# Which products of the first tile run on whole float32 operands, and a new order of the first 32 steps

## The chip, the cores and the metric

The kernel runs on one core of a Trainium2 chip, as one program with one launch. The metric is device time in microseconds, from the first to the last instruction with what the launch adds to it. The program is scheduled by a tool that writes each engine's instructions in a fixed order at build time; on the chip each engine goes through its own list in that order and waits for semaphores. The engines are named PE (matmuls; its weight loads are PEld), DVE (VectorE), ACT (ScalarE), POOL (GpSimd) and SP, whose queue issues nearly all DMAs here.

## The reference

Three stages follow each other; only the second is touched by the change.

```python
# 1: gated linear attention, 4 x 8 heads, 768 positions, head size 48
state = alpha[:, :, t, :, None] * state + einsum(k[:, :, t], v[:, :, t])
y[:, :, t] = einsum(q[:, :, t], state)
# 2: x is y as 3072 tokens x 384
h = x @ w_in                                  # 384 -> 2048
g = h * np.tanh(softplus(h))
x = g @ w_out                                 # 2048 -> 384
# 3: each token to the one expert of 8 with the largest logit
logits = x @ w_gate
out = gate * (np.maximum(x @ w1[e], 0.0) @ w2[e])
```

## The kernel before

**Attention units.** The 3072 tokens are cut into 24 units of 128 (unit u is u0, u1, ...). A unit is loaded by one DMA of 1 MB (`load_unit`, L339), goes through two scans and two products on DVE (`a_prep1`, `a_prep2`), a transpose on PE (`a_kt`), the products of q and k on PE with a masked copy `am` on DVE (`a_qk`), the sum `y` on PE (`a_y`), and the product that updates the state (`a_kv`). `a_y` ends in `xh`, a copy by ACT, and from the second tile on also in `xl`, what is left of float32 when `xh` is taken away, by DVE. `unit` has two buffers (unit 2 has one of its own), so the load of unit u+2 waits for `a_kv` of unit u on PE.

**Tiles and steps.** Three units make a tile of 384 tokens, 8 tiles in all. A tile is worked in 16 steps, one for each block f of 128 of the 2048 hidden columns. Step s (tile s // 16, block s % 16) is `mm1` (first product, into one of three PSUM buffers `h`), `act_tanh` and `act_mish` on ACT in batches of three steps, and six steps later `mm2` (second product, added up in `acc`). An `h` buffer is free when `tau` and the copy `hc` have been made from it: by ACT both in the first tile, `hc` by DVE (L659) in the others.

**Two ways of a product.** A float32 product is done either in one matmul with whole float32 operands, which PE runs as two recorded passes, or in three matmuls of the shorter type float32r on halves (high x high, high x low, low x high). Before, the first tile has whole operands in both products (L623 and L696), and the other seven have halves in both (L629, L701).

**Weights.** Block f of both weight matrices arrives as 64-bit numbers (`wraw`, 768 KB, two buffers, L346). `prep_w` makes float32 of them with three DVE instructions (`w_bits`, L66, L69, L72) into `wx[f]`. `prep_c` and `prep_d` turn the block of w_out on PE, multiply it with the gate's weights and put 8 more columns behind it (`wt`, `wot`, `wc`). `halve(f)` splits the whole of `wx[f]` into `w_h` (ACT, L429) and `wl` (DVE, L430), first at step 12.

**Order.** The first 32 steps or so follow a string of words written by hand: `a3` is `a_prep1(3)`, `b` `a_prep2`, `t` `a_kt`, `q` `a_qk`, `y` `a_y`, `v` `a_kv`, `l` a load, `w`, `c`, `d` the three preparations of a block, `m` a step, `s` `halve`, `z` one of four zero fills of `xs` (L799, 6.8 MB together), `P` the room for the second half of the weights. After the string a loop runs steps 16 on, with the later units between them. The words set the order in which the tool sees the work, and on SP's queue also the order of the DMAs. `craw` loads (L828) read the weights a second time for a check.

Of the kernel before, what the change touches and what calls it, by code (L numbers as in the profile page):

```python
# [18 lines left out]
P = 128  # L19
# [258 lines left out]
def kernel(ctx: ExitStack, tc: tile.TileContext, att, w_io, w_gate, w1, w2, out):  # L278
    nc = tc.nc
# [8 lines left out]
    s2p = s2.enter_context(tc.tile_pool(name="s2p", bufs=2))  # L288
# [6 lines left out]
    s0p = s0.enter_context(tc.tile_pool(name="s0p", bufs=2, side="right"))  # L295

    nc.scalar.preload_act_table_set("sigmoid_and_others")
    wt = {}

    def room_w(h, pool):  # L300
        wt[h] = pool, pool.tile([P, NF // 2, UO], F32R, tag="w_h", name="w_h")
        if h:
            wt["spare"] = pool

    wx = {}
    wl = {}

    def wt_f(f):
        return wt[f // (NF // 2)][1][:, f % (NF // 2)], wl[f]

    room_w(0, wpool)
    pre = ExitStack()
# [48 lines left out]
    ident = const.tile([P, P], F32, name="ident")  # L361
    nc.gpsimd.memset(ident, 1.0)
    nc.gpsimd.affine_select(
        out=ident, in_=ident, pattern=[[-1, P]], compare_op=ALU.is_equal, fill=0.0, base=0, channel_multiplier=1
# [4 lines left out]
        out=mask, in_=mask, pattern=[[1, P]], compare_op=ALU.is_ge, fill=0.0, base=0, channel_multiplier=-1  # L369
# [4 lines left out]
        out=before, in_=before, pattern=[[1, P]], compare_op=ALU.is_gt, fill=0.0, base=0, channel_multiplier=-1  # L374
# [26 lines left out]
    wot = {}  # L401

    def prep_w(f):
        wx[f] = wt[f // (NF // 2)][0].tile([P, UO], F32, tag=f"x{f}", name="wx", bufs=1)
        w_bits(nc, wx[f][:, 0:2 * DM].bitcast(I32), wraw.pop(f), False)
        load_w(f + 2)

    def prep_c(f):
        ps = ps_a.tile([P, 512], F32, tag="att", name="wt")
        for c in range(KC):  # L410
            nc.tensor.transpose(ps[:, c * P:(c + 1) * P], wx[f][:, DM + c * P:DM + (c + 1) * P], ident)
        wot[f] = s0p.tile([P, DM], F32, tag="wot", name="wot", bufs=1)
        nc.scalar.activation(out=wot[f], in_=ps[:, 0:DM], func=AF.Copy)

    def prep_d(f):
        wo = wot.pop(f)
        ps = ps_a.tile([P, 512], F32, tag="att", name="wc")
        for c in range(KC):
            nc.tensor.matmul(ps[:, 0:E], wo[:, c * P:(c + 1) * P], wg[:, c], start=(c == 0), stop=(c == KC - 1))
        nc.scalar.activation(out=wx[f][:, 2 * DM:], in_=ps[:, 0:E], func=AF.Copy)  # L420

    def halve(s):
        f = s - HALVE
        if 0 <= f < NF:
            x = wx.pop(f)
            pool, tag = (wt["spare"], "spare") if f == 0 else (wt[(f - 1) // (NF // 2)][0], f"x{f - 1}")
            wl[f] = pool.tile([P, UO], F32R, tag=tag, name="wl", bufs=1)
            h, l = wt_f(f)
            nc.scalar.activation(out=h, in_=x, func=AF.Copy)  # L429
            nc.vector.tensor_tensor(out=l, in0=x, in1=h.bitcast(F32), op=ALU.subtract)  # L430

    st = {}
    xt = {}
# [81 lines left out]
    def a_y(u):  # L515
        sc1, kc, qc, kn, am = st[u]
        v3 = unit_t[u][:, OV:].rearrange("p (h c) -> p h c", c=64)
        inter = u >= B
        ps = bank(u, "y")[:, 0:DM].rearrange("p (a b) -> p a b", b=P)
        parts = []  # L520
        for c in range(KC):
            cs = slice(0, 32) if c < 2 else slice(32, 64)
            for q in range(4):
                hs = [4 * c + q] if c < 2 else [2 * q, 2 * q + 1]
                mm = [(v3[:, h, cs], am[:, h // 2, h % 2]) for h in hs]
                if inter:
# [159 lines left out]
    def mm2(s):  # L686
        j, f = divmod(s, NF)
        gh, gl = live.pop(s)
        if j:
            wo_h, wo_l = (t[:, DM:] for t in wt_f(f))  # L690
        if f == 0:
            acc[j] = [ps_acc.tile([P, 512], F32, tag=f"acc{g}", name="acc") for g in range(G)]
        for g in range(G):
            gs = slice(g * P, (g + 1) * P)
            if j == 0:
                nc.tensor.matmul(  # L696
                    acc[j][g][:, 0:DM + E], gh[:, gs], wx[f][:, DM:], start=(f == 0), stop=(f == NF - 1)
                )
                continue
            for i, (l, w) in enumerate(((gh, wo_h), (gh, wo_l), (gl, wo_h))):  # L700
# [104 lines left out]
    def more_w(_):  # L805
# [286 lines left out]
```

## Time and profile before

| | |
|---|---|
| time, median of 3 runs (lowest to highest) | 887.9 us (885.42 to 888.7) |
| the profiled execution: its time, its span | 887.04 us, 885.3 us |
| mean granted TensorE clock | 0.968 |
| PE busy, PE weight loads busy | 94%, 83% of the span |
| DVE, ACT, POOL busy | 56%, 57%, 27% |

Shares are of the whole span. The profile cuts it into stretches too, and gives the clock that was granted to PE in each: 1.00 is 2.4 GHz, 0.50 is 1.2 GHz. Records of matmuls overlap, so the time that one takes is read from the distance between starts.

### The profile page before, as it was taken

To read this page: it belongs to the slowest core of one execution; us is meant where nothing else is said; L and a number is where in the kernel's file an instruction comes from. 1 tells how busy PE (TensorE), PEld (TensorE's weight loads), DVE (VectorE), ACT (ScalarE), POOL (GpSimd) and SP (SyncE) were. 2 spreads that over 40 slices of the span, in tenths; PEclk is the share of its full clock that TensorE was granted. 3 is DMA by queue.
4 is the path that set the end of the run, shared out by engine and by line. 5 is a ranking of instruction groups with operands and counts; after the bars stand their busy time and mean duration, and the time that the engine had idled before them with its cause. 6 is when DMAs were issued, how large, how long until landed. Compare 5 with 4: busy or idle time off the path is not lost. (4 is left out here: it accounts for less than half of the span.)

```text
span 885.3 us, 14754 instructions
## 1 busy us (share of the span) xinstructions
PE 829.4 (94%) x5892; PEld 738.5 (83%) x5892; DVE 495.0 (56%) x955; ACT 507.1 (57%) x782; POOL 240.0 (27%) x290
## 2 busy tenths in 40 slices
PE   7697889999999999999999999994899999999994
PEld 4464557899999989999999999894799999999994
DVE  7985446575776667676665644743543553354220
ACT  1294526756765866676757867883543554455231
POOL 2100011164354354254354342252001101100111
PEclk9798879999999999999999999998899999999997
DMA  7568515131342342332121102200833553353001
GB/s 285 203 208 242 153 48 165 50 110 49 119 148 85 120 147 84 120 111 85 49 76 49 49 29 82 62 28 29 271 108 125 165 170 116 118 186 116 27 30 33
DMA packets 24313, 98.41 MB, mean 111 GB/s; under 512 B 3488, under 2 KB 9268, under 8 KB 21292
## 3 DMA queue, kind: packets, MB, share of 16 engines
q1 hardware_dynamic: 20652, 87.89, 30.9%
q0 software_dynamic: 3584, 9.50, 3.1%
q8 instruction: 48, 0.79, 0.4%
q14 instruction: 29, 0.24, 0.1%
HBM read 80.93 MB, written 17.03 MB: 111 GB/s over the span
## 5 line engine op out<-in xcount | busy, mean ns | idle before, releaser
L683 POOL TENSOR_TENSOR gl<-tau,gh 128x384 fp32r<-128x384 f32 x110 | 113.5, 1040 | 165.5 <-ACT gh L681 129.6
L929 PE MATMUL g<-eh,ew 128*128 128x432 f32 x384 | 119.0, 364 | 0.0
L629 PE MATMUL h<-xh,w_h 128*128 128x384 f32 x336 | 117.0, 350 | 0.9 <-DVE hc L659 0.9
L701 PE MATMUL acc<-w_h,gh 128*128 128x392 f32 x336 | 116.1, 346 | 1.0 <-ACT gh L681 0.7
L701 PE MATMUL acc<-wl,gh 128*128 128x392 f32 x336 | 115.0, 342 | 0.0
L629 PE MATMUL h<-xl,w_h 128*128 128x384 f32 x336 | 114.9, 342 | 0.0
L701 PE MATMUL acc<-w_h,gl 128*128 128x392 f32 x336 | 112.2, 345 | 2.6 <-POOL gl L683 2.6
L629 PE MATMUL h<-xh,wl 128*128 128x384 f32 x336 | 114.6, 341 | 0.0
L655 ACT ACTIVATE tau<-h 128x384 f32<-128x384 f32 x128 | 61.1, 492 | 88.9 <-PE h L629 53.9
L680 DVE TENSOR_TENSOR tau<-tau,hc 128x384 f32<-128x384 f32 x112 | 73.4, 707 | 68.1 <-ACT tau L670 40.0
L974 PE MATMUL y<-hh,ew 128*128 128x432 f32 x336 | 105.3, 364 | 1.0 <-ACT hh L933 1.0
L943 POOL DMA_INDIRECT out_dram<-yo,xg x32 | 31.8, 993 | 228.3 <-ACT yo L942 207.4
L934 DVE SCALAR_TENSOR_TENSOR hl<-g,hh 128x432 fp32r<-128x432 f32 x64 | 38.8, 605 | 93.5 <-ACT hh L933 93.5
L611 DVE TENSOR_TENSOR ew<-est,ew 128x512 fp32r<-128x512 f32 x96 | 64.3, 720 | 31.9 <-ACT ew L610 31.6
L933 ACT ACTIVATE hh<-g 128x432 fp32r<-128x432 f32 x64 | 33.6, 525 | 84.4 <-PE g L929 83.9
L681 ACT ACTIVATE gh<-tau 128x384 fp32r<-128x384 f32 x112 | 58.4, 524 | 39.9 <-PE acc L701 20.8
L929 PEld LDWEIGHTS g<-eh,ew 128*128 128x128 f32 x384 | 72.8, 190 | 3.5
L610 ACT ACTIVATE ew<-est 128x512 fp32r<-128x512 f32 x92 | 51.6, 623 | 31.8 <-PE g L929 16.8
L929 PE MATMUL g<-el,ew 128*128 128x432 f32 x192 | 69.5, 362 | 0.0
L659 DVE COPY hc<-h 128x384 f32<-128x384 f32 x112 | 59.9, 546 | 15.2 <-ACT tau L655 15.1
L629 PEld LDWEIGHTS h<-xh,w_h 128*128 128x128 f32 x336 | 63.1, 188 | 5.0 <-DVE hc L659 1.2
L701 PEld LDWEIGHTS acc<-w_h,gl 128*128 128x128 f32 x336 | 62.6, 188 | 4.0 <-POOL gl L683 3.1
(144 smaller groups left out, 1651.1 us busy)
## 6 DMA issues: line engine op xcount, KB each, us to landing
unit<-in_att_dram SPq DMA_DIRECT2D x23, 1026.5 KB
est<-in_w_dram SPq DMA_DIRECT2D x28, 768.0 KB
wraw<-in_w_io_dram SPq DMA_DIRECT2D x16, 768.0 KB
craw<-in_w_io_dram SPq DMA_DIRECT2D x16, 768.0 KB
xs<-zrow SPq DMA_DIRECT2D x3, 1746.0 KB
xg<-xs SPq DMA_DIRECT2D x7, 654.8 KB
est<-in_w_dram SPq DMA_DIRECT2D x4, 512.0 KB
xs<-zrow SPq DMA_DIRECT2D x1, 1552.0 KB
```

The costliest lines, as they stand in the source:

```text
L610: nc.scalar.activation(out=th[:, cs], in_=tx, func=AF.Copy)
L611: nc.vector.tensor_tensor(out=tl[:, cs], in0=tx, in1=th[:, cs].bitcast(F32), op=ALU.subtract)
L629: nc.tensor.matmul(ps, l[:, k], r[:, k], start=(n == 0), stop=(n == 3 * KC - 1))
L655: nc.scalar.activation(out=t[:, i], in_=hbuf[s], func=AF.Tanh, scale=0.5)
L659: copied[:] = [nc.vector.tensor_copy(out=h[:, i], in_=hbuf.pop(s))]
L680: nc.vector.tensor_tensor(out=t[:, x], in0=t[:, x], in1=h[:, x], op=ALU.mult)
L681: nc.scalar.activation(out=gh, in_=t[:, x], func=AF.Copy)
L683: eng.tensor_tensor(out=gl, in0=t[:, x], in1=gh.bitcast(F32), op=ALU.subtract)
L701: nc.tensor.matmul(acc[j][g][:, 0:DM + E], l[:, gs], w, start=(f == 0 and i == 0), stop=(f == NF - 1 and i == 2))
L929: nc.tensor.matmul(ps, l[:, k, fs], r[:, k], start=(n == 0), stop=(n == 3 * KC - 1))
L934: nc.vector.scalar_tensor_tensor(out=hl, in0=ps, scalar=0.0, in1=hh.bitcast(F32), op0=ALU.max, op1=ALU.subtract)
L974: nc.tensor.matmul(yac[e][c], l[:, f, cs], r, start=(f == 0 and i == 0), stop=(f == NF2 - 1 and i == 2))
```

## The change

In the first tile `mm1` now runs on halves like in the other tiles; `mm2` keeps whole operands there. `prep_w` therefore makes float32 into a buffer `wbits` of two, and from it `wi_h` (ACT), `wi_l` (DVE) and a float32 copy of the w_out part `wx` (ACT); `a_y` makes `xh` and `xl` in the first tile too. `halve` is left with the w_out part (392 columns in place of 776), four steps later in the program's words. `wot` moves to three buffers shared with `gl`. In the string the units 3 to 6 stand earlier, and the zero fills z0 and z1 later.

```diff
-HALVE = 12
+HALVE = 16
@@ prep_w
-        wx[f] = wt[f // (NF // 2)][0].tile([P, UO], F32, tag=f"x{f}", name="wx", bufs=1)
-        w_bits(nc, wx[f][:, 0:2 * DM].bitcast(I32), wraw.pop(f), False)
+        raw = wraw.pop(f)
+        t = s0p.tile([P, 2 * DM], I32, tag="wbits", name="wbits", bufs=2)
+        tf = t.bitcast(F32)
+        w_bits(nc, t, raw, False)
+        ih, il = (x.rearrange("p k m -> p (k m)") for x in wt_f(f)[0:2])
+        nc.scalar.activation(out=ih, in_=tf[:, 0:DM], func=AF.Copy)
+        nc.vector.tensor_tensor(out=il, in0=tf[:, 0:DM], in1=ih.bitcast(F32), op=ALU.subtract)
+        wx[f] = wt[f // (NF // 2)][0].tile([P, DM + E], F32, tag=f"wo{f}", name="wx", bufs=1)
+        nc.scalar.activation(out=wx[f][:, 0:DM], in_=tf[:, DM:], func=AF.Copy)
@@ prep_c
-        wot[f] = s0p.tile([P, DM], F32, tag="wot", name="wot", bufs=1)
+        wot[f] = s2p.tile([P, DM], F32, tag="gl", name="wot", bufs=KB)
@@ a_y
-        xh, xl = (t and t[:, :, o * P:(o + 1) * P] for t in xt[j])
-        if j == 0:
-            nc.scalar.activation(out=xh, in_=ps, func=AF.Copy, scale=1.0 / SCALE)
-            return
+        xh, xl = (t[:, :, o * P:(o + 1) * P] for t in xt[j])
@@ mm1
-        if j == 0:
-            for k in range(KC):
-                nc.tensor.matmul(ps, wx[f][:, k * P:(k + 1) * P], xh[:, k], start=(k == 0), stop=(k == KC - 1))
-            return
@@ the string of words
-        "a0 b0 t0 q0 a1 b1 h4 t1 q1 y0 v0 h4 l3 a2 b2 h2 t2 q2 w0 y1 h4 v1 y2 v2 l4 w1 m0 c0 a3 w2 m1 P d0 c1 b3 w3 "
+        "a0 b0 t0 q0 a1 b1 h4 t1 q1 y0 v0 h4 l3 a2 b2 h2 t2 q2 w0 y1 h4 v1 y2 v2 l4 w1 a3 b3 m0 c0 t3 q3 w2 "
...
```

**DVE after the second masked copy of unit 2.** DVE's rows before, from the two `am` of unit 2 on (`sc_411` belongs to unit 3, `sc_527` to unit 4):

```order
L511 TENSOR_TENSOR am<-qk,mask 128x4x128
L452 RECIPROCAL rc<-rc 128x4
L511 TENSOR_TENSOR am<-qk,mask 128x4x128
L69 SCALAR_TENSOR_TENSOR wx<-wraw,wx 128x768
L453 SCALAR_TENSOR_TENSOR rst_102<-sc_411,rc 128x4
L442 SCALAR_TENSOR_TENSOR sc_527<-unit,rst_101 128x516
```

In the changed kernel DVE has `am` of unit 2, then the first scan of unit 4 (`sc_523`), and then these rows down to `xl` of unit 2:

```order
L71 SCALAR_TENSOR_TENSOR wbits<-wraw,wbits 128x768
L463 SCALAR_TENSOR_TENSOR rst_104<-sc_411,rc 128x4
L65 TENSOR_SCALAR wbits<-wraw 128x768
L459 TENSOR_SCALAR rc<-sc_523 128x4
L479 TENSOR_TENSOR unit<-unit,sc_523 128x512
L569 COPY s<-kv 128x256
L466 SCALAR_TENSOR_TENSOR sc_412<-unit,rst_104 128x516
L68 SCALAR_TENSOR_TENSOR wbits<-wraw,wbits 128x768
L413 TENSOR_TENSOR wi_l<-wbits,wi_h 128x384
L462 RECIPROCAL rc<-rc 128x4
L480 TENSOR_TENSOR unit<-unit,sc_412 128x512
L552 SCALAR_TENSOR_TENSOR xl<-y,xh 128x3x128
```

Before, nothing on DVE stood between the first tile's `y` and its `mm1`; now `xl` of unit 2 does, thirteen rows behind `am` of unit 2.

**DVE around the scan of unit 7.** Before (`sc_1167` and `sc_1168` are the scans of unit 7, the `hc` are those of tile 1, whose first one frees the `h` of step 16):

```order
L564 TENSOR_TENSOR s<-kv,sp 128x256
L659 COPY hc<-h 128x384
L675 TENSOR_TENSOR gh<-tau,hc 128x384
L430 TENSOR_TENSOR wl<-wx,w_h 128x776
L442 SCALAR_TENSOR_TENSOR sc_1167<-unit,rst_101 128x516
L659 COPY hc<-h 128x384
```

In the changed kernel (`sc_1323` and `sc_1324` are the scans of unit 7):

```order
L762 MEMSET row 128x3x2
L571 TENSOR_TENSOR s<-kv,sp 128x256
L678 TENSOR_TENSOR gh<-tau,hc 128x384
L440 TENSOR_TENSOR wo_l<-wx,wo_h 128x392
L452 SCALAR_TENSOR_TENSOR sc_1323<-unit,rst_103 128x516
L678 TENSOR_TENSOR gh<-tau,hc 128x384
L459 TENSOR_SCALAR rc<-sc_1323 128x4
L462 RECIPROCAL rc<-rc 128x4
L463 SCALAR_TENSOR_TENSOR rst_104<-sc_1323,rc 128x4
L440 TENSOR_TENSOR wo_l<-wx,wo_h 128x392
L466 SCALAR_TENSOR_TENSOR sc_1324<-unit,rst_104 128x516
L662 COPY hc<-h 128x384
```

The first `hc` of tile 1 stood ahead of unit 7's first scan and now stands seven rows behind it.

**SP's queue.** SP's DMAs before, from the third `wraw` but one on (the `unit` in the first row is unit 4; the three later ones are 5, 6 and 7):

```order
L339 DMA unit<-in_att_dram 128x2053
L346 DMA wraw<-in_w_io_dram 128x768 x9
L799 DMA xs<-zrow 128x8x388
L346 DMA wraw<-in_w_io_dram 128x768 x3
L799 DMA xs<-zrow 128x9x388 x2
L339 DMA unit<-in_att_dram 128x2053 x3
L799 DMA xs<-zrow 128x9x388
L828 DMA craw<-in_w_io_dram 128x768 x2
```

In the changed kernel, from unit 4 on (the next `unit` rows are 5 and 6; 7 is the first of the last row):

```order
L342 DMA unit<-in_att_dram 128x2053
L349 DMA wraw<-in_w_io_dram 128x768 x7
L342 DMA unit<-in_att_dram 128x2053
L349 DMA wraw<-in_w_io_dram 128x768 x3
L342 DMA unit<-in_att_dram 128x2053
L349 DMA wraw<-in_w_io_dram 128x768 x2
L801 DMA xs<-zrow 128x8x388
L801 DMA xs<-zrow 128x9x388 x3
L830 DMA craw<-in_w_io_dram 128x768 x2
L342 DMA unit<-in_att_dram 128x2053 x4
```

Units 5 and 6 now stand among the weights; all four zero fills stand together behind the last weights, and unit 7 stands behind them and behind two `craw`.

## Rows read from the trace of the kernel before

**Rows 1.** The page: the granted clock in 40 equal slices of the span.

```profile
PEclk9798879999999999999999999998899999999997
```

**Rows 2.** Busy time in stretches: length, five engines, clock, DMA share, GB/s.

```profile
36.40:70.00 33.60, 33.38 (x133) 20.47 (x132) 28.60 (x41) 25.41 (x39) 0.00 (x0) 1.00 0.65 215
70.00:77.40 7.40, 2.60 (x12) 1.26 (x8) 1.93 (x4) 6.04 (x9) 0.00 (x0) 1.00 1.02 290
77.40:84.20 6.80, 6.24 (x45) 4.49 (x46) 6.39 (x9) 3.35 (x6) 0.00 (x0) 0.50 0.34 76
84.20:104.70 20.50, 17.13 (x97) 11.23 (x95) 10.10 (x17) 10.30 (x17) 0.22 (x1) 1.00 0.82 241
104.70:115.00 10.30, 9.41 (x71) 6.23 (x71) 3.57 (x6) 3.39 (x7) 0.00 (x0) 0.50 0.01 2
115.00:125.20 10.20, 8.10 (x58) 5.45 (x57) 6.26 (x11) 3.34 (x7) 3.08 (x3) 1.00 0.31 103
125.20:132.00 6.80, 5.52 (x66) 4.25 (x66) 2.79 (x4) 1.41 (x3) 1.18 (x1) 0.50 0.01 2
132.00:178.60 46.60, 46.12 (x318) 37.80 (x318) 26.07 (x56) 32.50 (x50) 7.99 (x9) 1.00 0.40 116
```

**Rows 3.** PE in order of time: start us, us, engine line, records, idle before.

```profile
34.60 5.67 PE L623 MATMUL h<-xh,wx 128*128 128x384 f32 x14
...
85.80 4.03 PE L623 MATMUL h<-xh,wx 128*128 128x384 f32 x12
89.67 0.38 PE L411 MATMUL wt<-ident,wx 128*128 128x128 f32 x2
...
168.16 0.34 PE L629 MATMUL h<-xl,w_h 128*128 128x384 f32 x1
...
169.56 0.34 PE L701 MATMUL acc<-w_h,gh 128*128 128x392 f32 x1
...
178.62 0.18 PE L738 MATMUL rank<-ecap,ones 128*128 128x8 bf16 x1
```

**Rows 4.** DVE in order of time, between the second `am` of unit 2 and unit 3's products.

```profile
30.84 0.66 DVE L511 TENSOR_TENSOR am<-qk,mask 128x512 f32<-128x512 f32 x1
31.41 0.95 DVE L69 SCALAR_TENSOR_TENSOR wx<-wraw,wx 128x768 int32<-128x768 int32 x1
32.28 0.16 DVE L453 SCALAR_TENSOR_TENSOR rst<-sc,rc 128x4 f32<-128x4 f32 x1
32.35 1.23 DVE L442 TENSOR_TENSOR_SCAN sc<-unit,rst 128x516 f32<-128x516 f32 x1
33.49 0.40 DVE L562 COPY s<-kv 128x256 f32<-128x256 f32 x1
...
37.33 0.68 DVE L470 TENSOR_TENSOR unit<-unit,sc 128x512 f32<-128x512 f32 x1
```

**Rows 5.** Waits, in order of time: DVE, then PE.

```profile
76.74 0.56 DVE L66 TENSOR_SCALAR wx<-wraw 128x768 int32<-128x768 int32 x1 [5.47 <-DMA wraw<-in_w_io_dram]
...
101.94 1.23 DVE L442 TENSOR_TENSOR_SCAN sc<-unit,rst 128x516 f32<-128x516 f32 x1 [2.53 <-DMA unit<-in_att_dram]
...
77.96 1.45 PE L419 MATMUL wc<-wg,wot 128*128 128x8 f32 x6 [3.52 <-DVE am L511]
...
105.59 0.81 PE L533 MATMUL y<-unit,sp 64*32 64x128 f32 x9 [3.68 <-ACT wx L420]
```

**Rows 6.** SP's DMA issues: start us.

```profile
62.92 0.43 SPq L799 DMA_DIRECT2D xs<-zrow  x1
...
81.11 1.14 SPq L799 DMA_DIRECT2D xs<-zrow  x2
...
90.81 0.35 SPq L339 DMA_DIRECT2D unit<-in_att_dram  x1
```

**Rows 7.** Stretches in which mostly zero fills moved, then one with a unit.

```profile
84.00:97.00 13.00, 12.88 (x68) 8.29 (x66) 5.59 (x8) 3.50 (x7) 0.00 (x0) 0.99 1.06 298
...
118.00:120.50 2.50, 2.38 (x16) 1.86 (x15) 0.47 (x1) 1.98 (x4) 0.00 (x0) 1.00 0.77 325
```

More of the change, by code (lines that the diff above doesn't have):

```diff
@@ L47 @@
 UW = OV + UV
-UO = 2 * DM + E
 LAG = 6
-HALVE = 12
+HALVE = 16
 SCALE = 2.0 ** 27
@@ L300, in room_w @@
     def room_w(h, pool):
-        wt[h] = pool, pool.tile([P, NF // 2, UO], F32R, tag="w_h", name="w_h")
-        if h:
-            wt["spare"] = pool
+        n = NF // 2
+        wt[h] = (
+            pool,
+            pool.tile([P, n, KC, P], F32R, tag="wi_h", name="wi_h"),
+            pool.tile([P, n, KC, P], F32R, tag="wi_l", name="wi_l"),
+            pool.tile([P, n, DM + E], F32R, tag="wo_h", name="wo_h"),
+        )
     wx = {}
-    wl = {}
+    wo_l = {}
     def wt_f(f):
-        return wt[f // (NF // 2)][1][:, f % (NF // 2)], wl[f]
+        return [t[:, f % (NF // 2)] for t in wt[f // (NF // 2)][1:]]
     room_w(0, wpool)
@@ L410, in prep_c @@
         for c in range(KC):
-            nc.tensor.transpose(ps[:, c * P:(c + 1) * P], wx[f][:, DM + c * P:DM + (c + 1) * P], ident)
-        wot[f] = s0p.tile([P, DM], F32, tag="wot", name="wot", bufs=1)
+            nc.tensor.transpose(ps[:, c * P:(c + 1) * P], wx[f][:, c * P:(c + 1) * P], ident)
+        wot[f] = s2p.tile([P, DM], F32, tag="gl", name="wot", bufs=KB)
         nc.scalar.activation(out=wot[f], in_=ps[:, 0:DM], func=AF.Copy)
@@ L419, in prep_d @@
             nc.tensor.matmul(ps[:, 0:E], wo[:, c * P:(c + 1) * P], wg[:, c], start=(c == 0), stop=(c == KC - 1))
-        nc.scalar.activation(out=wx[f][:, 2 * DM:], in_=ps[:, 0:E], func=AF.Copy)
+        nc.scalar.activation(out=wx[f][:, DM:], in_=ps[:, 0:E], func=AF.Copy)
     def halve(s):
@@ L425, in halve @@
             x = wx.pop(f)
-            pool, tag = (wt["spare"], "spare") if f == 0 else (wt[(f - 1) // (NF // 2)][0], f"x{f - 1}")
-            wl[f] = pool.tile([P, UO], F32R, tag=tag, name="wl", bufs=1)
-            h, l = wt_f(f)
+            pool, tag = (wt[1][0], "spare") if f == 0 else (wt[(f - 1) // (NF // 2)][0], f"wo{f - 1}")
+            wo_l[f] = pool.tile([P, DM + E], F32R, tag=tag, name="wo_l", bufs=1)
+            h = wt_f(f)[2]
             nc.scalar.activation(out=h, in_=x, func=AF.Copy)
-            nc.vector.tensor_tensor(out=l, in0=x, in1=h.bitcast(F32), op=ALU.subtract)
+            nc.vector.tensor_tensor(out=wo_l[f], in0=x, in1=h.bitcast(F32), op=ALU.subtract)
     st = {}
@@ L536, in a_y @@
             xt[j] = (
-                s2p.tile([P, KC, TT], F32R if j else F32, tag="xh", name="xh", bufs=2),
-                s2p.tile([P, KC, TT], F32R, tag="xl", name="xl", bufs=2) if j else None,
-            )
-        xh, xl = (t and t[:, :, o * P:(o + 1) * P] for t in xt[j])
-        if j == 0:
-            nc.scalar.activation(out=xh, in_=ps, func=AF.Copy, scale=1.0 / SCALE)
-            return
+                s2p.tile([P, KC, TT], F32R, tag="xh", name="xh", bufs=2),
+                s2p.tile([P, KC, TT], F32R, tag="xl", name="xl", bufs=2),
+            )
+        xh, xl = (t[:, :, o * P:(o + 1) * P] for t in xt[j])
         nc.scalar.activation(out=xh, in_=ps, func=AF.Copy, scale=1.0 / SCALE)
@@ L618, in mm1 @@
         xh, xl = xt[j]
+        wi_h, wi_l = wt_f(f)[0:2]
         ps = ps_h.tile([P, 512], F32, tag="h", name="h")[:, 0:TT]
-        hbuf[s] = ps
-        if j == 0:
-            for k in range(KC):
-                nc.tensor.matmul(ps, wx[f][:, k * P:(k + 1) * P], xh[:, k], start=(k == 0), stop=(k == KC - 1))
-            return
-        wi_h, wi_l = (t[:, 0:DM].rearrange("p (k m) -> p k m", m=P) for t in wt_f(f))
         n = 0
@@ L630, in mm1 @@
                 n += 1
+        hbuf[s] = ps
     live = {}
@@ L688, in mm2 @@
         gh, gl = live.pop(s)
-        if j:
-            wo_h, wo_l = (t[:, DM:] for t in wt_f(f))
+        wh = wt_f(f)[2]
         if f == 0:
@@ L696, in mm2 @@
                 nc.tensor.matmul(
-                    acc[j][g][:, 0:DM + E], gh[:, gs], wx[f][:, DM:], start=(f == 0), stop=(f == NF - 1)
+                    acc[j][g][:, 0:DM + E], gh[:, gs], wx[f], start=(f == 0), stop=(f == NF - 1)
                 )
                 continue
-            for i, (l, w) in enumerate(((gh, wo_h), (gh, wo_l), (gl, wo_h))):
+            for i, (l, w) in enumerate(((gh, wh), (gh, wo_l[f]), (gl, wh))):
                 nc.tensor.matmul(
@@ L811 @@
         "a": a_prep1, "b": a_prep2, "t": a_kt, "q": a_qk, "y": a_y,
-        "v": a_kv, "l": load_unit, "w": prep_w, "c": prep_c, "d": prep_d, "h": warm, "s": halve, "m": step, "z": zero, "P": more_w
+        "v": a_kv, "l": load_unit, "w": prep_w, "c": prep_c, "d": prep_d, "h": warm, "m": step, "z": zero, "P": more_w
     }
```

6 rows, old and new, of the table does are left out of this document.

## The prediction

> **What bounds the kernel now.** First the clock line of the page [rows 1]: PE has its full clock from the sixth of 40 slices to the end of the seven tiles, and not before. With PE 94% busy over the span, the first 130 us or so are where time can be found. The stretches [rows 2] show how much. Here PE's idle time is the length less the busy time; I add it up over the eight rows and get 142.2 - 128.5 = 13.7 us. In three of them (6.8 + 10.3 + 6.8 = 23.9 us) the clock is 0.50 and PE is busy for 21.2 us, in which it does 10.6 us of full-speed work: another 10.6 us lost.
>
> From the rank matmuls of the first tile's routing on, PE's list is the same in both kernels, row for row to the last. Before, they begin at 178.62 us [rows 3]; from there PE is busy without a break. So I ask only when the changed kernel gets there: what it gains by that mark is the gain of the whole.
>
> What holds PE before the mark is read from the waits [rows 5, 6]. DVE sits 5.47 us for a `wraw`, behind the zero fill that SP put into the DMA queue at 62.92 us, and PE then waits 3.52 us for an `am` that stands behind it on DVE. Later unit 5 is issued at 90.81 us, when `a_kv` of unit 3 frees its buffer, and lands at 101.94 behind two more zero fills issued at 81.11. Tile 1's `mm1` needs unit 5, so PE has only `mm2` of the first tile for a while, waits 3.68 us for a small copy, and gets the half clock twice more.
>
> **PE's work.** Twelve records of a whole-operand `mm1` take 85.80 to 89.67, 0.322 us a record and 0.645 a matmul. Eight of the halves take 168.16 to 169.56, 0.175 each [rows 3]. Removed: 16 steps x 3 x 0.645 = 31.0 us. Added: 16 x 9 x 0.175 = 25.2 us. PE gains 5.8 us at the full clock. `mm2` of the first tile stays.
>
> All of PE's rows from the first `mm1` at 34.60 to the mark, at such distances: 31.0 for `mm1`, 31.6 for the first tile's `mm2` (48 x 0.658), 20.5 for the 117 matmuls of tile 1, and 32.3 for units and weights, together 115.4 us of the 144.0 us that pass. The 28.6 us lost are the 13.7 idle, the 10.6 at half clock, 0.9 more at half clock before 36.4, and 3.4 that I can't place.
>
> **The start.** Before, `am` of unit 2 ends at 31.5 on DVE [rows 4], `y` and `xh` follow, and `mm1` begins at 34.60. Changed, DVE has three `wi_l` and two `xl` more ahead of `am` of unit 2. No 384-column subtraction to float32r has a row here; copying from the nearest, the product of 512 columns at 0.68 [rows 4], I take 0.47, at least 0.3 and at most 0.68. Five make 2.3 us; with about 1.4 us for a `wraw` that comes later by as much, `am` ends at 35.2. Then `xl` of unit 2 waits its turn behind two scans (1.15 each, from 32.35 to 33.49), two long bit operations (0.87, from 31.41 to 32.28), a short one (0.5), two products (0.6 each), a `wi_l`, a copy and three tiny ones: 6.8 us, and `xl` itself makes it 42.5. PE meanwhile has unit 3's `qk`, which stands ahead and takes about 3 us at half clock once unit 3's product is there. So the first matmul with `xl` runs at **45.0** (41 to 48), 10 us later than the first `mm1` now, and 1.5 us more go to the half clock. The 2.5 us of unit 3 and the first three matmuls are done by then; left to the mark are 115.4 - 5.8 - 2.5 = **107.1 us** of PE work.
>
> **What holds PE on the way.** DVE must have each block's `wi_l` ready. From 42.5 to the bits of block 13 it has about 39 us of work: ten blocks of bits at 2.2 us, nine `wi_l`, four `wo_l`, six `gh`, unit 5's preparation, and small things. Add 6 us of waits for `wraw`, as each is asked for only when a buffer is free, and it is there at about 88. PE has by then nearly the same amount to do, and I find it late once, for `wi_l` of block 10: **4.5 us** (0 if DMA is quicker, 10 if every wait adds up). ACT has two copies of 384 and one of 392 for one of 776 before: some 0.4 us more per step, with 8 of 33.6 us idle [rows 2], so I take nothing, at most 6 us. `xh` of unit 5 stands behind a table load and a `wo_h` on ACT: **1.6 us** (0 to 4).
>
> **The zero fills.** SP issues them all after the last `wraw`, at about 89. They are 1552 + 3 x 1746 KB, 6.95 MB. The two of before moved, with the tail of a `wraw`, at 298 GB/s, other DMAs' share included [rows 7], so 24 to 26 us from about 93, when the last weights have landed: 118. Two `craw` (1.57 MB, 5 us) and unit 7 (1.05 MB, 3 us) come behind them: unit 7 lands at 125 (121 to 133). DVE goes through its list in order; behind unit 7's scan stand `hc` of step 16 (3.6 us later, 128.7), and with it PE's matmuls of step 19, which need that buffer of `h`. PE gets there at 45.0 + 70.4 + 1.5 + 4.5 + 1.6 = 123. It waits **5 us** (0 to 14). After idle time of this size the clock was 0.50 for 6.8 and 10.3 us [rows 2, 5], so I take **3.5 us** for that (0 to 10), and **3 us** (0 to 5) for what I couldn't place before.
>
> The packet size of the zero fill (1,552 bytes) is smaller than a unit's, and the Trainium skill (DMA: Bandwidth & Descriptors, section on why small descriptors are slow) puts it down to a fixed overhead of about 3 beats for each packet. Estimated from that page, 48.5 + 3 beats is 6% more, and at 325 GB/s less 6% the zero fills end 2 to 3 us sooner than by the row of 298; the sum would be about 169 instead of 171. The row decides here, and its rate is the one used.
>
> **The sum.** 45.0 + 1.5 + 107.1 + 4.5 + 1.6 + 5 + 3.5 + 3 = 171.2 us against 178.6: 7.4 us sooner. The profiled execution took 887.04 us, 0.9 below the median; less 7.4 that is 879.6.
>
> **The rivals.** *No hold at the zero fills* (chance 0.22): unit 7 lands by 119, say because SP issues sooner. Then the 5 + 3.5 us fall away, 16 us sooner, **871**. For it: the zero fills of before moved at 298 GB/s with the engines full; against it: two `craw` stand in front of unit 7.
>
> *Unit 7 comes so late that it decides* (0.14): each us that its scan starts after 119.5 holds PE for one. Break-even with before is reached at about 132. If weights arrive slowly at first, the zero fills start 5 us later and move at 260 GB/s (27 us), the scan is at 137, PE stands still for 17 us with the half clock behind it: 887.0 - 7.4 + 12 = **891.5**. For it: DVE waited 5.47 us behind a zero fill a quarter as long [rows 5, 6]. Against: DVE's earlier rows would have to be late while PE isn't.
>
> *The clock falls as often as before* (0.08): the first `h<-xl` late by 10 us, `wi_l` late at several blocks and the stop at unit 7 each end in a stretch at 0.50, three in all as before, which cost 10.6 us [rows 2], where the sum has 1.5 and 3.5. That is 5.6 us more with nothing else changed, 879.6 + 5.6 = **885.2**. The trace shows such falls only after waits of 3.5 us and more [rows 2, 5], and I expect one such wait, not three. The Trainium skill (TensorE: Matmul & The Clock Gate, on oscillation) speaks for this rival: it says that a matmul engine which micro-idles again and again between groups of matmuls goes back and forth between the two levels; here this is borne out as far as three falls in 60 us go.
>
> *Nothing to be seen* (0.12): the later start (10.4 us) and the new waits eat the 5.8 us of matmuls and the idle time alike, and the time is **886**. This is the case if DVE, 28.6 of 33.6 us busy already [rows 2] and given 0.47 more a step in the chain, sets the pace to the end of the tile, 6 us worse than I have it.
>
> **How the numbers follow.** The forecast has 0.44, with a range of its own of 875 to 884. Under 0.5%, about 4.4 us, no measurement of this kernel tells a change from none, so faster means below 883.5, slower above 892.3. Of the forecast 0.39 is faster and 0.05 the same; the first rival (0.22) is faster; the second (0.14) is half slower, half the same; the third is 0.02 faster and 0.06 the same; the fourth 0.09 the same and 0.03 slower. That gives faster 0.63, same 0.27, slower 0.10. The range of 868 to 890 leaves out the slow 0.08 of the second rival, and some 0.1 at both ends for sizes beyond my bounds.
>
> **What would show it.** In the changed profile: `mm1` of the first tile at 0.175 us a matmul; the first `h<-xl` near 45 us; no DVE wait over 3 us for a `wraw`; tile 1's first `mm1` near 108 (134 before); a DVE wait for unit 7's DMA that ends near 125, a PE wait for `hc` near 123 to 129, and the half clock after it; the first rank matmul near 171. I am wrong if PE waits for `wi_l` at many blocks, if the zero fills are through before DVE needs unit 7, or if the clock is at half more often than once between 50 and 120 us.

## The result and the profile after

The changed kernel takes **878.42 us** (median of 4 runs, 876.6 to 879.1) against 886.66 us for the kernel before beside it: a ratio of 0.9896, with a 95% interval of 0.9871 to 0.9921 (the two medians alone give 0.9907). The forecast was 879.6. The profiled execution took 878.88 us (span 877.1), 8.2 us less than that of before.

The clock line of the page; beside it stands [rows 1]:

```profile
PEclk9699889999999999999999999997899999999998
```

Busy time in stretches cut where the clock changes, after the first; length, five engines, clock, DMA share, GB/s, as in [rows 2]:

```profile
0.00:50.00 50.00, 33.17 (x300) 23.68 (x301) 43.72 (x75) 12.95 (x27) 6.72 (x50) 0.83 0.60 219
50.00:97.50 47.50, 42.42 (x326) 33.43 (x325) 42.45 (x67) 41.53 (x74) 4.44 (x5) 1.00 0.69 232
97.50:100.90 3.40, 3.40 (x6) 1.40 (x5) 2.83 (x5) 1.08 (x3) 0.00 (x0) 0.50 1.07 315
100.90:107.70 6.80, 5.33 (x40) 4.76 (x39) 1.84 (x3) 5.56 (x9) 0.00 (x0) 1.00 1.06 303
107.70:114.50 6.80, 5.69 (x60) 3.88 (x61) 1.12 (x2) 3.38 (x6) 0.00 (x0) 0.50 1.08 254
114.50:168.40 53.90, 53.90 (x360) 43.37 (x359) 26.30 (x61) 33.61 (x60) 8.96 (x10) 1.00 0.22 70
```

From 114.5 us on PE has no idle time and the full clock; before, the full clock came back at 132 us, with 0.5 us idle behind it [rows 2].

PE in order of time, as in [rows 3]: the first product with `xl`, three halves in a row, the four waits of over 1 us behind 46 us, the first product of tile 1, the first product of step 19 and the first rank matmul.

```profile
43.45 0.69 PE L631 MATMUL h<-xl,wi_h 128*128 128x384 f32 x1
...
74.91 1.16 PE L512 MATMUL qk<-unit 64*128 64x128 f32 x14 [1.27 <-ACT wot L423]
...
87.32 0.34 PE L631 MATMUL h<-xh,wi_h 128*128 128x384 f32 x1
87.50 0.34 PE L631 MATMUL h<-xl,wi_h 128*128 128x384 f32 x1
87.68 0.34 PE L631 MATMUL h<-xh,wi_l 128*128 128x384 f32 x1
...
89.74 0.45 PE L631 MATMUL h<-xh,wi_l 128*128 128x384 f32 x1 [1.37 <-DVE wi_l L413]
...
96.28 0.45 PE L631 MATMUL h<-xh,wi_h 128*128 128x384 f32 x1 [1.19 <-ACT wi_h L412]
...
108.81 1.66 PE L543 MATMUL y<-unit,sp 64*32 64x128 f32 x24 [2.58 <-ACT wx L430]
...
115.96 0.60 PE L631 MATMUL h<-xh,wi_h 128*128 128x384 f32 x2
...
130.86 0.34 PE L631 MATMUL h<-xh,wi_h 128*128 128x384 f32 x1
...
168.44 0.18 PE L740 MATMUL rank<-ecap,ones 128*128 128x8 bf16 x1
```

The mark of the prediction, the first rank matmul, comes at 168.44 us: 10.2 us sooner than before [rows 3], where 7.4 were forecast. Of these 8.2 are left at the end. Most of the difference, 1.8 us, goes near 385 us, far behind every edit. There DVE waits for an earlier scatter of POOL to finish with its rows; DVE's row of that wait, first of the kernel before, then of the changed one:

```profile
392.59 0.17 DVE L757 COPY row<-ids 128x3 int32<-128x3 int32 x1 [4.30 <-DMA xs<-row,slot]
```

```profile
383.91 0.17 DVE L759 COPY row<-ids 128x3 int32<-128x3 int32 x1 [6.17 <-DMA xs<-row,slot]
```

The wait is 1.87 us longer, and two waits of PE stand behind it (0.78 for an `s` and 1.22 for an `xl` on DVE). No edit touches this place, and PE, DVE, ACT and POOL have the same order there in both kernels: the wait has another length, the lists are no others.

### The profile page after: what moved, and what is told of

Its sections match the earlier page's. It is cut to its first block, busy times and chain, and to the rows that moved or that the text cites. A ratio compares the mean times of both kernels' runs of the same rounds, so it can differ in the third digit from the quotient of the medians.

```text
span 877.1 us, 14907 instructions
## 1 busy us (share of the span) xinstructions
PE 820.3 (94%) x5940; PEld 741.9 (85%) x5940; DVE 497.2 (57%) x974; ACT 513.8 (59%) x814; POOL 238.4 (27%) x290
## 5 line engine op out<-in xcount | busy, mean ns | idle before, releaser
L686 POOL TENSOR_TENSOR gl<-tau,gh 128x384 fp32r<-128x384 f32 x110 | 113.4, 1038 | 176.8 <-ACT gh L684 129.4
L631 PE MATMUL h<-xh,wi_h 128*128 128x384 f32 x384 | 134.6, 353 | 2.5 <-ACT wi_h L412 1.4
L631 PE MATMUL h<-xh,wi_l 128*128 128x384 f32 x384 | 132.6, 345 | 1.4 <-DVE wi_l L413 1.4
L631 PE MATMUL h<-xl,wi_h 128*128 128x384 f32 x384 | 130.8, 341 | 0.0
L703 PE MATMUL acc<-wo_h,gh 128*128 128x392 f32 x336 | 116.1, 346 | 1.1 <-ACT gh L684 0.6
L703 PE MATMUL acc<-wo_l,gh 128*128 128x392 f32 x336 | 115.2, 343 | 0.0
L703 PE MATMUL acc<-wo_h,gl 128*128 128x392 f32 x336 | 112.2, 345 | 2.7 <-POOL gl L686 2.7
L631 PEld LDWEIGHTS h<-xh,wi_h 128*128 128x128 f32 x384 | 72.6, 190 | 7.5 <-ACT wi_h L412 2.0
L631 PEld LDWEIGHTS h<-xh,wi_l 128*128 128x128 f32 x384 | 72.6, 189 | 3.4 <-DVE wi_l L413 1.9
L631 PEld LDWEIGHTS h<-xl,wi_h 128*128 128x128 f32 x384 | 72.7, 189 | 1.1 <-DVE rst L463 0.2
```

The source lines that it names most:

```text
L686: eng.tensor_tensor(out=gl, in0=t[:, x], in1=gh.bitcast(F32), op=ALU.subtract)
L703: nc.tensor.matmul(acc[j][g][:, 0:DM + E], l[:, gs], w, start=(f == 0 and i == 0), stop=(f == NF - 1 and i == 2))
```

## The experiments

Three times are read in each trace: the mark, what is lost before it, and what passes from the last rank matmul to the end of the span. **Lost** is PE's idle time plus half of its busy time at clock 0.50, both added up from busy times in stretches. In the changed kernel, for instance, from 46.3 us to the mark: idle 5.08 + 1.47 + 1.11 = 7.7, and (3.40 + 5.69) / 2 = 4.5. **Rest** is the mark less the lost time, so PE's work at the full clock with its small gaps. The marks, lost times and rests are of one execution each; the ratios are of 4 to 12 runs beside runs of the kernel before on the same chip.

| kernel | ratio to before, 95% interval | mark | lost before it (of it up to 50 us) | rest | behind the last rank matmul |
|---|---|---|---|---|---|
| before | 1 | 178.6 | 39.4 (15.1) | 139.2 | 275.5 |
| the change | 0.9896 [0.9871, 0.9921] | 168.4 | 34.4 (22.2) | 134.0 | 276.0 |
| e1 halves, old order | 0.9996 [0.9978, 1.0014] | 176.8 | 41.7 (20.1) | 135.1 | 278.7 |
| e2 whole, new order | 1.0014 [0.9993, 1.0035] | 173.5 | 34.9 (15.0) | 138.6 | 279.6 |
| e3 zero fills early | 0.9946 [0.9928, 0.9965] | 171.8 | 36.8 (22.3) | 135.0 | 275.4 |
| e4 whole products | 0.9993 [0.9978, 1.0009] | 175.0 | 35.0 (18.6) | 140.0 | 275.3 |
| e5 low halves on POOL | 0.9964 [0.9947, 0.9980] | 172.7 | 36.8 (19.3) | 135.9 | 275.9 |
| e6 copy on DVE | 0.9889 [0.9871, 0.9908] | 167.3 | 35.1 (22.2) | 132.2 | 276.3 |
| e7 both | 0.9895 [0.9871, 0.9919] | 168.1 | 33.9 (20.3) | 134.2 | 277.2 |
| e8 as e2, one warm more | 0.9925 [0.9899, 0.9952] | 168.4 | 28.9 (12.9) | 139.5 | 275.6 |
| e9 the change, one warm more | 0.9878 [0.9850, 0.9905] | 166.1 | 31.4 (21.7) | 134.7 | 275.6 |
| e10 before, zero fills late | 0.9962 [0.9944, 0.9980] | 175.2 | 35.7 (14.9) | 139.4 | 274.9 |
| e11 as e9, few low halves | 0.9922 [0.9894, 0.9950] | 166.9 | 32.8 (17.9) | 134.1 | 276.3 |
| e12 before, one warm more | 1.0001 [0.9976, 1.0026] | 174.7 | 34.8 (15.2) | 139.9 | 278.0 |

**e1: the halves without the order.** The changed kernel with the string of before (its `s12` to `s15` fall away, as `prep_w` does that work now):

```
-        "... w1 a3 b3 m0 c0 t3 q3 w2 m1 P d0 c1 y3 a4 w3 ..."
+        "... w1 m0 c0 a3 w2 m1 P d0 c1 b3 w3 m2 d1 c2 t3 w4 ..."
```

> The changed kernel with the order of before (units and zero fills where they stood): halves alone. If the products and the order each give a part (my theory): 5.8 us of matmuls fall away, and the wait for weights behind the first zero fill (5.5 us on DVE before) and the late unit 5 stay, so 880 to 884 us, some 2 to 6 us above the changed kernel. If the order alone gave the gain: 885 to 889, as the new work on DVE then meets the old stalls. If the products alone gave it: 877 to 880.

Measured: 885.85 us, no change. PE's work is 4 us less, but 5 us more are lost before 50 us, and the half clock takes more than before: 16.3 us up to the mark, where it took 13.7.

**e2: the order without the halves.** The kernel of before with the string of the change, and its own `s` behind the steps (shown against the string of the change):

```
-        "m12 d11 c12 w14 z0 z1 m13 d12 c13 w15 m14 d13 c14 z2 m15 d14 c15 d15 z3"
+        "m12 s12 d11 c12 w14 z0 z1 m13 s13 d12 c13 w15 m14 s14 d13 c14 z2 m15 s15 d14 c15 d15 z3"
```

> The kernel of before with the order of the change, its first tile's first products still whole: the order alone. My theory: the zero fills hold no weights, the half clock falls less often, and some 3 us of the gain come, 882 to 885 us. If the order gave all of it: 877 to 880. If the products alone gave it, or the order without the halves costs something: 886 or more.

Measured: 887.56 us, no change. So in these two builds neither part alone gives anything that can be measured, and both together give 1%: my theory that two gains are added is not borne out by them (e8 shows how far that hangs on the build). And the trace has the mark 5.2 us sooner than before, and loses 4.1 us of it behind the last rank matmul. The instructions there were not edited, yet their order is another: the scheduler that lays out each engine's list dealt it otherwise. ACT at the entry of the experts, in order of time, first in the kernel before, then in e2:

```profile
625.17 0.53 ACT L912 ACTIVATE eh<-t 128x432 fp32r<-128x432 f32 x1 [0.94 <-PE t L909]
628.37 1.68 ACT L610 ACTIVATE ew<-est 128x512 fp32r<-128x512 f32 x3 [2.67 <-DMA est<-in_w_dram]
629.95 0.51 ACT L912 ACTIVATE eh<-t 128x432 fp32r<-128x432 f32 x1
630.36 0.52 ACT L933 ACTIVATE hh<-g 128x432 fp32r<-128x432 f32 x1
```

```profile
621.18 0.53 ACT L912 ACTIVATE eh<-t 128x432 fp32r<-128x432 f32 x1 [0.94 <-PE t L909]
625.15 1.67 ACT L610 ACTIVATE ew<-est 128x512 fp32r<-128x512 f32 x3 [3.44 <-DMA est<-in_w_dram]
626.73 0.51 ACT L912 ACTIVATE eh<-t 128x432 fp32r<-128x432 f32 x1
628.04 1.67 ACT L610 ACTIVATE ew<-est 128x512 fp32r<-128x512 f32 x3 [0.80 <-DMA est<-in_w_dram]
629.62 0.93 ACT L933 ACTIVATE hh<-g 128x432 fp32r<-128x432 f32 x2
```

From the third `eh` to the first `hh`, for which PE waits, there are 5.2 us before and 8.4 in e2, as `hh` stands behind a second batch of `ew` there.

**e3: the zero fills early again,** units and halves as in the change:

```
-        "m6 d5 c6 q5 w8 ... v5 l7 w10 ... w14 z0 z1 m13 ..."
+        "m6 d5 c6 q5 z0 w8 ... v5 l7 z1 w10 ... w14 m13 ..."
```

> The changed kernel with z0 and z1 named where before had them, so that the first zero fill is issued ahead of unit 5 and of the weights of the last blocks, and the last behind unit 7. If the zero fills' place carries the part of the order (my theory): a DVE wait of 3 to 6 us for a wraw is back, PE waits behind it, and the time is 880 to 884. If only the units' place matters: 877.5 to 879.5, no difference. If the late zero fills cost something in the changed kernel (PE's wait near 106 us): 874 to 877.

Measured: 881.51 us, 0.5% over the change, as expected in size but by another way: no wait for a `wraw` is back. The loss comes at unit 7. SP's issues, DVE's wait for the unit and PE's wait behind it:

```profile
120.74 0.33 SPq L342 DMA_DIRECT2D unit<-in_att_dram  x1
121.12 0.43 SPq L801 DMA_DIRECT2D xs<-zrow  x1
```

```profile
127.53 1.23 DVE L452 TENSOR_TENSOR_SCAN sc<-unit,rst 128x516 f32<-128x516 f32 x1 [2.92 <-DMA unit<-in_att_dram]
```

```profile
130.59 0.44 PE L631 MATMUL h<-xh,wi_h 128*128 128x384 f32 x1 [1.49 <-ACT hc L660]
```

A zero fill is issued 0.4 us behind the unit and can share the transfers with it; the unit's scan starts at 127.53, and in the changed kernel at 125.44; 0.6 of these 2.1 us are the later issue. They are enough for PE to stand still, but one step ahead of the place that the prediction named and by another path. Step 18 waits for the `h` of step 15, which ACT frees by its `hc`; ahead of that stands a `tau` that waited for a `gh` of DVE, and this `gh` stands behind the unit's scan:

```profile
129.66 0.49 ACT L658 ACTIVATE tau<-h 128x384 f32<-128x384 f32 x1 [2.86 <-DVE gh L678]
130.05 0.48 ACT L660 ACTIVATE hc<-h 128x384 f32<-128x384 f32 x1
```

At step 19, which the prediction named, PE loses 0.3 us, by the distance between starts.

**e4: the products alone undone.**

```
+        if j == 0:
+            for k in range(KC):
+                nc.tensor.matmul(ps, wi_h[:, k].bitcast(F32), xh[:, k].bitcast(F32), start=(k == 0), stop=(k == KC - 1))
+            hbuf[s] = ps
+            return
```

> The changed kernel with the first tile's first products as 48 whole float32 matmuls of the high halves alone (the low halves of the weights and of x are made, but left out of these products); all else stays. PE has 5.8 us more to do at the full clock. If PE's work bounds that stretch: 883 to 885. If the waits that the changed kernel has before 110 us (7 us idle and some 5 us of half clock) take most of it in: 878 to 881.

Measured: 885.18 us, 6.8 above the change; the mark is 6.5 us later and the rest 6.0 us longer. In the new order PE's work is paid for in full.

**e5, e6, e7: two repairs of the changed kernel.** e5 gives the first low halves to POOL, e6 takes the small copy off ACT, e7 does both:

```
-        nc.vector.tensor_tensor(out=il, in0=tf[:, 0:DM], in1=ih.bitcast(F32), op=ALU.subtract)
+        (nc.gpsimd if f < 8 else nc.vector).tensor_tensor(out=il, in0=tf[:, 0:DM], in1=ih.bitcast(F32), op=ALU.subtract)
...
-        nc.scalar.activation(out=wx[f][:, DM:], in_=ps[:, 0:E], func=AF.Copy)
+        nc.vector.tensor_copy(out=wx[f][:, DM:], in_=ps[:, 0:E])
```

> The changed kernel with the low halves of the weights of the first 8 blocks made on POOL (about 1.04 us each there, as its other products of 384) and not on DVE (0.47). If the work that the change puts on DVE ahead of the first low half of x sets the start (my theory): the first h<-xl some 1.5 us sooner than 43.45 and the time 1 to 2.5 us less than the changed kernel's, 876 to 877.5. If it is paid back by PE waiting for slower low halves from POOL: 879 to 882. If the start is not what counts, as a later wait (the small copy behind the tables near 106 us, unit 7) takes the gain: 878 to 879.

> The changed kernel with the copy of 8 columns behind each wc made on DVE, not on ACT, where one stood behind three table loads and passes and held PE for 2.6 us at 106 us, with the half clock behind it (6.8 us). If that wait is a loss of its own: 2.6 + 3.3 us less, 872 to 875. If unit 7 then holds PE as I had forecast for the change (its buffer is freed by the same PE work, the zero fills end at 118): 875 to 878. If the copy on DVE waits behind long work there and PE with it: 879 or more.

> Both edits on the changed kernel: the low halves of the first 8 blocks on POOL, the small copies on DVE. If their gains add: 870 to 874. If unit 7 bounds the end of the stretch: 874 to 877, no better than the better one of the two.

Measured: 884.74, 878.55 and 878.87 us, on a chip where the kernel before took 888.46. e5 loses 0.7% against the change, though it loses 2.9 us less before 50 us: 6.3 us are lost between 50 and 100 us in the change and 9.3 in e5, and 5.9 and 8.2 behind that. POOL took 1.0 to 1.9 us for each of its eight low halves, half of them 1.3 or more, where I had 1.04. e6 takes the wait at 106 us away, and the time behind 100 us loses only 3.4 us, but the same copy now stands in DVE's list and the loss from 50 to 100 us is 9.5 us. Three of PE's waits in e6 between 70 and 101 us:

```profile
75.00 0.45 PE L631 MATMUL h<-xh,wi_h 128*128 128x384 f32 x1 [1.64 <-ACT wi_h L412]
76.72 0.45 PE L631 MATMUL h<-xh,wi_l 128*128 128x384 f32 x1 [1.10 <-DVE wi_l L413]
...
100.11 2.07 PE L512 MATMUL qk<-unit 64*128 64x128 f32 x14 [1.79 <-DVE wx L430]
```

e7 is no better than the change either. Each wait taken away was replaced by another, so I asked what the waits hang on (e11).

**e8, e12, e9: the same string with one warming matmul more.** One more `h` makes ACT's order at the experts' entry that of before again in the order-alone kernel (it runs near 19 us, not near 26 as the expectations say):

```
-        "... h4 l3 a2 b2 h2 t2 q2 ..."
+        "... h4 l3 a2 b2 h3 t2 q2 ..."
```

> The kernel of before with the order of the change, and one more warming matmul on PE near 26 us, which makes ACT's and DVE's order at the entry of the experts that of before again (the order alone had another there, with hh of the first expert later). If the order alone was 5 us sooner at the first rank matmul and lost it at the experts' entry: the entry takes 32 us as before and the time is 880 to 883.5. If its time was right as it stood (the order alone gives nothing): 886 to 889.

> The kernel of before with the extra warming matmul alone. Its list at the start is dealt a little otherwise on PE, DVE and ACT, and at the experts' entry ACT has hh of the first expert later, as the order alone had it when it was no faster. If that entry costs some 4 us (36.3 us against 32.0 there): 1.003 to 1.007 of before, with the entry over 35 us. If the entry is not the cause: 0.997 to 1.002. If one warming matmul itself brought the gain of the order alone: 0.993 or less.

> The changed kernel with the same extra warming matmul near 26 us as the run with the order alone had; every other instruction stands in the same order as in the changed kernel. It is the partner of that run: both have the new order and the extra matmul, this one has the halves too. If the halves gain 5 us also beside the better start: 0.983 to 0.986 of before. If the halves' work on DVE at the start eats what their products save, once the order is as good: 0.988 to 0.991, as the changed kernel, and within 3 us of the order alone (0.9925).

Measured: e8 881.48 us beside a before of 888.46; behind the last rank matmul it takes 275.6 us, as before, and it is 0.75% faster. But its mark too is 5.1 us sooner than that of e2, which I had not expected: with the extra matmul the start is dealt otherwise as well. e12 shows the same in the old order: its mark is 4.0 us sooner than before, 2.5 us of which go again behind the last rank matmul, and its time is that of before; my 0.3 to 0.7% for the entry's order are seen in the trace and not in the time. So e12 and e8 are a pair with equal products, and so are before and e2: the order is worth 6.3 us at the mark in the one and 5.2 in the other. In time it is 0.76% in the first pair (1.0001 to 0.9925) and nothing in the second; the entry's order gives 2.4 us of that in the first pair and takes 4.1 us in the second. So the zero of e2 was that of one build. One warming matmul moved the mark by 2.3 to 5.1 us, as much as either part of the change does; e1 was not built with it, so whether the halves alone gain in another build of the old order stays open. e8 and e9 are the pair for the halves in the new order: the rest is 4.8 us shorter, 2.5 us more are lost, and the time goes from 0.9925 to 0.9878, with intervals that overlap. e9 has the lowest ratio of all; whether it beats the change (0.9896) these runs don't tell.

**e10: the zero fills alone,** in the kernel of before:

```
-        "... q5 z0 w11 ... v5 l7 z1 w13 ... w14 m13 ..."
+        "... q5 w11 ... v5 l7 w13 ... w14 z0 z1 m13 ..."
```

> The kernel of before with z0 and z1 moved to where the change has them, all four zero fills behind the last wraw; units and products as before. The prediction put the wait of 5.5 us on DVE, PE's waits of 3.5 and 3.7 us and two stretches of half clock down to the zero fills ahead of weights and of unit 5. If that is right: no DVE wait over 3 us for a wraw, unit 5 lands some 8 us sooner, and 3 to 6 us less, 0.993 to 0.9965 of before. If the zero fills were only what the trace named last and the units' place counts: 0.998 to 1.002.

Measured: 0.38% faster (883.48 beside 887.35). The longest DVE wait for a `wraw` is 1.0 us, where it was 5.47 [rows 5], and PE's wait for `am` is 0.46, where it was 3.52. But PE's other wait, 3.68 for the small copy, is still there:

```profile
99.38 1.66 PE L533 MATMUL y<-unit,sp 64*32 64x128 f32 x24 [3.67 <-ACT wx L420]
```

Nor does unit 5 come sooner. SP's issues of e10, and DVE in order of time:

```profile
73.72 12.34 SPq L799 DMA_DIRECT2D xs<-zrow  x4
86.64 48.55 SPq L339 DMA_DIRECT2D unit<-in_att_dram  x3
```

```profile
102.39 0.17 DVE L757 COPY row<-ids 128x3 int32<-128x3 int32 x1 [9.19 <-DMA xs<-zrow]
104.77 1.23 DVE L442 TENSOR_TENSOR_SCAN sc<-unit,rst 128x516 f32<-128x516 f32 x1 [2.20 <-DMA unit<-in_att_dram]
```

All four zero fills stand ahead of unit 5, whose scan starts at 104.77 (101.94 before, [rows 5]), and DVE waits 9.19 us for the zero fills themselves at `row<-ids`, a row that the prediction did not look at. The units' earlier place is the other half of the order: with it units 5 and 6 are ahead of the zero fills, and the wait at that row is 0.87 us in the changed kernel (below).

**e11: the start without its low halves,** otherwise e9:

```
-        nc.vector.tensor_tensor(out=il, ...)
+        if f >= 3:
+            nc.vector.tensor_tensor(out=il, ...)
...
+        xl = xl if j else xh
+        wi_l = wi_l if f >= 3 else wi_h
```

> The changed kernel with the extra warming matmul, without DVE's low halves of x for the first tile and of the weights of blocks 0 to 2 (the high halves stand in for them, so the output leaves these low parts out); PE has the same number of matmuls. Against its partner with all low halves it shows what DVE's work at the start costs. If the start that comes 10 us later is paid in full at the end (lost time up to 50 us was 22.2 us in the changed kernel, 14.9 in before): first h<- matmuls with the second operand near 36 us and 5 to 8 us less, 0.980 to 0.984 of before. If later waits take most of it, as they did when low halves went to POOL: 0.986 to 0.990.

Measured: 880.55 us, 0.9922, no faster than its partner e9. Up to 50 us it loses 3.8 us less than e9 (17.9 for 21.7); from 50 to 100 us it loses 9.7, where e9 loses 4.8. Three of PE's waits there:

```profile
70.06 0.44 PE L636 MATMUL h<-xh,wi_l 128*128 128x384 f32 x1 [1.18 <-DVE wi_l L414]
...
74.87 1.01 PE L636 MATMUL h<-xh,wi_h 128*128 128x384 f32 x2 [1.92 <-ACT wi_h L412]
...
95.34 0.44 PE L636 MATMUL h<-xh,wi_l 128*128 128x384 f32 x1 [1.44 <-DVE wi_l L414]
```

A start that is sooner brings PE sooner to weights that are not ready. In the changed kernel DVE is busy for 42.45 of the 47.5 us from 50 us on and ACT for 41.53 (the stretches above): the start does not set the pace there. That the making of the weights (their bits and their halves) on these two engines does is argued from these shares and waits, not tested by itself.

## Where the prediction held and where it failed

The forecast case came, 1.2 us off, but that the number is so near is in part luck: the hold at the zero fills (5 us and 3.5 us of half clock) did not come, and idle time, half clock and small gaps that the sum did not have made up for nearly all of it.

- **PE's work** was forecast 5.8 us shorter. The halves run at the 0.175 us a matmul of [rows 3] (87.32 to 87.68 is two), and the rest falls by 5.2 us; e4 makes it 6.0 us longer again. Right, with the condition that e1 adds: it pays only where PE is the bound.
- **The start:** the first `h<-xl` at 45.0 forecast, 43.45 measured, and the half clock behind it took 1.4 us (to 46.3) where I had 1.5. Right as a time. As a cost it is nearly empty: e11 loses 3.8 us less there than e9 and reaches the mark no sooner.
- **What holds PE on the way:** 4.5 for `wi_l` and 1.6 for `xh` forecast, and nothing for ACT's other copies. Measured from 46.3 us to the mark are 7.7 us of idle time: 1.37 for a `wi_l`, none for `xh`, and 6.2 that end with ACT (2.58 at 108.81 for `y`, 1.27 and 0.69 for a `wot`, 1.19 for a `wi_h`, two under 0.3). So the term that I put at nothing was the largest. `y` needs the bank from which ACT copies the 8 columns of `wc`, and that copy stands behind ACT's table loads, in order of time:

```profile
104.62 1.28 ACT L671 ACT_TABLE_LOAD   x1
105.92 1.25 ACT L671 ACTIVATE tau<-tau,half 128x1152 f32<-128x1152 f32 x1
107.19 1.28 ACT L672 ACT_TABLE_LOAD   x1
108.48 0.18 ACT L430 ACTIVATE wx<-wc 128x8 f32<-128x8 f32 x1
```

  The prediction had read this wait in the kernel before (3.68 us, [rows 5]), put it down to the late unit 5, and left it out of the sum. It is 2.1 to 3.7 us in every kernel here that has the copy on ACT, wherever the units and zero fills stand.

- **The zero fills** are the step that failed. I had them end at 118, unit 7 land at 125, and PE wait 5 us for the `hc` behind its scan, with 3.5 us of half clock. DVE in order of time:

```profile
118.35 0.17 DVE L759 COPY row<-ids 128x3 int32<-128x3 int32 x1 [0.87 <-DMA xs<-zrow]
...
125.44 1.23 DVE L452 TENSOR_TENSOR_SCAN sc<-unit,rst 128x516 f32<-128x516 f32 x1 [1.41 <-DMA unit<-in_att_dram]
...
130.12 0.53 DVE L662 COPY hc<-h 128x384 f32<-128x384 f32 x1
```

  Both times are right to half a microsecond, and PE waits for nothing there. One of my signs of being wrong is met: the zero fills are through 5.7 us before DVE comes to the scan of unit 7 (at 124.03, with its wait of 1.41 us still ahead). Nor is it the queue that makes unit 7 late. SP's issues:

```profile
86.83 14.14 SPq L801 DMA_DIRECT2D xs<-zrow  x4
101.07 6.24 SPq L830 DMA_DIRECT2D craw<-in_w_io_dram  x2
120.15 44.76 SPq L342 DMA_DIRECT2D unit<-in_att_dram  x2
```

  The unit is issued at 120.15, when the `kv` of unit 5 has freed its buffer, behind zero fills that were already done. PE itself was late: it comes to step 19 at 130.86, where I had 123, with 12.2 us of idle time and half clock behind it since 46.3 us, where I had 6.1; the `hc` was done 0.2 us before. As the unit waits for PE's `kv`, a PE that comes sooner also brings the unit sooner: e9, with the same lists but for one matmul, issues it at 117.01 and its scan starts at 123.10. e3 shows that a hold behind the scan is real at 2.1 us more, though by another path. That the queue would have held the unit had PE been on time, 8 us sooner, was not tried. By the estimate from the Trainium skill (DMA: Bandwidth & Descriptors, on small descriptors) the zero fills would have ended 2 to 3 us sooner; in the trace they end at 118.3, as by the row's rate.
- **The clock:** I expected one fall behind 50 us and called more than one a sign of being wrong; there are two, with 1.7 and 2.8 us lost, 4.5 where I had 3.5. With the one at the start that is three, as that rival had it, but behind the first `h<-xl` they cost 5.9 us, where the sum had 5.0 and the rival 10.6 (up to the mark 9.9, 13.7 before). The fall at 97.5 comes 1.2 us behind a wait of 1.19 us (96.28, above). So my reading that falls come only after waits of 3.5 us and more does not hold, nor did it in the kernel before, where the fall at 125.2 us [rows 2] has this wait:

```profile
126.48 1.45 PE L419 MATMUL wc<-wg,wot 128*128 128x8 f32 x6 [3.26 <-DVE am L511]
```

- **The sum** from the first `h<-xl` to the mark: 4.5 + 1.6 + 5 + 3.5 + 3 = 17.6 us of losses forecast; measured 168.44 - 43.45 - 107.1 - 1.4 = 16.5, of which 7.7 idle, 4.5 by the clock and 4.3 that I can't place. The hold of 5 us fell away, and the others came out 1.6, 1.0 and 1.3 us larger. That is why the 871 of the first rival did not come, though its hold did not either. With the start 1.5 us sooner the mark came 2.8 us sooner than forecast.
- **That the gain at the mark is that of the whole** was wrong by 2.0 us, and it is the weaker premise. PE is not busy without a break behind the mark: at the experts' entry it waits 9.2 us for a DMA in both kernels. PE's list is the same from there on in the change, but ACT's and DVE's needn't be. In e1, e2 and e12 the time behind the last rank matmul is 2.5 to 4.1 us longer than before; in e2 and e12 the trace shows the list (there three of PE's `y` stand elsewhere too), in e1, whose lists there are those of before, a later landing of the first expert's weights (ACT waits 4.29 us for `est`).

The prediction's reason for the order, that zero fills hold weights, is borne out by e10 for the waits for `wraw` and `am`, and for 0.38% of the time; the wait for the small copy did not change with the zero fills' place. That their place would also bring unit 5 sooner is not shown by moving zero fills; it takes the units' new place (its scan starts at 70.39 us in the changed kernel).

## What to carry to other kernels

Work taken from the busiest engine pays only where nothing else sets its pace, so try it with the stalls in place and with them gone: here the halves were worth nothing in the old order (e1), and in the new one some 4 us with the work that they put on DVE and ACT (e8 to e9) and 6.5 us at the mark without it (e4). Where a scheduler lays out the lists, an edit at the start deals the end anew; read the time between two marks that no edit touches before putting a result down to the edit, and build each kernel in more than one dealing. Here each wait that was taken away on an engine fed by two others, 87 and 89% busy, came back a few microseconds on.

## What the hardware showed that I had not expected

The change and e9 have the same list on every engine but for one warming matmul near 19 us, and the half clock covers 27.3 us up to the mark in the one and 17.1 in the other. The stretches at 0.50 are 29.2 to 46.3, 97.5 to 100.9 and 107.7 to 114.5 in the change, and 29.1 to 35.9, 39.3 to 46.2 and 107.6 to 111.0 in e9. In the change the falls at 29.2 and 107.7 begin inside waits of PE, of 4.53 and 2.58 us, and the one at 97.5 shortly behind a wait of 1.19 us. The Trainium skill (TensorE: Matmul & The Clock Gate, on oscillation) tells of a kernel in which PE idles briefly between groups of matmuls so often that its clock goes back and forth between the two levels; the trace agrees as far as these places go. But lists that are alike up to one matmul gave 10 us more or less of half clock, in one execution each. No two traces of one and the same list were taken; the twelve runs of e1, one kernel, lie between 882.7 and 889.6 us, the two fastest with a mean granted clock of 0.971 and 0.969 and the two slowest with 0.962, so there too the clock goes with the time.
